# Attention, a dense layer pair and a top-2 mixture of experts on one core: loads, router tables, preparations and score products moved around the first pass

## The chip, the cores and the metric

One core of a Trainium2 chip runs the whole kernel as one program. The metric is device time in microseconds (us) of that program. Several executions are timed and their median counts; one more execution is profiled.

## The reference, cut to what matters

Three stages follow each other: causal attention with a decay (4 batches, 8 heads, 576 tokens, head size 64), a dense layer pair with squared ReLU (2304 tokens, 512 to 2048 to 512), and a router that sends each token to two of eight experts.

```
scores = q @ k.T / 8 + (cum[:, None] - cum[None, :])      # cum = cumsum(log f); causal
x = softmax(scores) @ v                                   # 2304 x 512
x = relu(x @ w_in) ** 2 @ w_out
logits = x @ w_gate + log1p(exp(x @ w_noise)) * noise
for each token: the two best experts, out += weight * (relu(x @ w1[e]) @ w2[e])
```

## The kernel before, in words

Most products run as three half-precision products (high times high, high times low, low times high), so an operand is first split into a high and a low part. ScalarE (ACT) copies the high part and VectorE (DVE) subtracts to get the low part.

**The ramp** is written out by hand: the string PLAN (line 57) is a list of tokens, and each issues one small step; the engines keep that order. It computes the "head" attention, which is the first two blocks of 128 queries of each batch, cut into 12 subs (numbered j, line 375). Per sub: S (hd_s, line 389) the scores, R (hd_max) the maxima, E (hd_exp) the exponentials, T, C and P the turn and the product with the values, n, h, l and XT the normalized tokens into xT. Subs 0 to 7 stand in PLAN, and j of 8 to 11 run later (hd_tick, line 520). The tokens lw0 to lw7 load the weight blocks of the dense layer on the queue of SyncE (SP), LW8 to LW11 on that of GpSimd (POOL); each is 1 MB and goes into one of two buffers (tag "w64"), which comes free when the block is converted (ca, cb, cc, ch, cl: conv_shift to conv_low, lines 549 to 568).

**The passes** (line 1087) are the dense layer. A pass takes one chunk c of 384 tokens through some of the 16 weight blocks i: mm1 (line 607) is 12 matmuls into the one PSUM tile m1, then ACT's ReLU, square and second square (lines 594 to 598) and DVE's low part (line 603); mm2 (line 636) is 9 matmuls into three accumulators, two steps later (LAG). Passes 0 and 1 do blocks 0 to 7 of chunks 0 and 1, and their sums are spilled to DRAM (spill, line 624, tiles sp) and fetched again (unspill, line 632, tile bk); passes 2 and 3 do blocks 8 to 15; then the other four chunks follow. Pass 0 is in PLAN (tokens m, r, g, a). From pass 1 on (after line 1086) a scheduler sets the order on every engine. It places instructions by priorities and its own estimates, and `with tc.issue_after(x)` tells it to put what stands inside behind x on the same engine. `pin` holds such instructions.

**In pass 1** hd_tick runs subs 8 to 11 beside the dense layer: hd_s (lines 394 to 412) makes two PSUM banks, one for each half z of the partitions. All its matmuls read 64 rows: z = 0 reads partitions 0 to 63, z = 1 partitions 64 to 127. The program writes them in turn, z = 0, z = 1, and so on. hd_split (line 496) then issues a transposing DMA (tile pt, line 504), and hd_pv16 (line 517) multiplies with the values.

**The rest of the attention** runs as 48 units (att_tick, line 954) beside passes 2 to 6. Before a pair of heads p of batch b can be used, load_qk (line 104, tile qkr, 896 KB, two buffers) and load_v (line 98, tile vr, 320 KB) fetch it on SP, and prep and prep_v (lines 192 and 207) split it: three ACT instructions (lines 199, 200, 212), three on DVE (201, 202, 213), and two small DMAs on POOL (205). Pairs 0 and 1 of batch 0 are loaded in pass 1, steps 4 and 5 (line 1141), but put only behind the last head turn of the ramp (token O7); all four preparations of batch 0 stand in the first ticks, which are in pass 2.

**The router's tables** are made by router_setup (line 673), called in pass 1 at step 1: two loads (wgr, nz), six constants on POOL, and two index tables (ini, ino) that POOL fills and SP writes to DRAM in three DMAs of 1024 short pieces each. Its three tiles and those of spill and of the turns share one set of three buffers (tag "x2").

After the passes, each expert is two layers on TensorE (PE) over gathered tokens.

## Time and profile before

| | |
|---|---|
| median of 3 runs | 962.51 us (961.18 to 967.23) |
| the profiled execution | 968.69 us |
| its span, first to last instruction | 966.6 us |
| mean granted TensorE clock | 0.992 |
| PE busy | 930.9 us |
| DVE, ACT, POOL busy | 569.0, 444.4, 203.9 us |

The first matmul of pass 0 starts at 43.9 us, that of pass 1 at 88.7 us and that of pass 2 at 133.7 us; the passes end at 542 us and the experts follow. A "wait" is idle time of an engine just before an instruction, put down to what ended it. In the timeline a row is a run of equal instructions on one engine: start, length, engine, line, operation, tiles, shape, count, and in brackets the idle time before it. Rows with a "q" behind the engine are the sequencer's DMA issues.

### The profile page before, as it was taken

To read this page: it belongs to the slowest core of one execution; us is meant where nothing else is said; L and a number is where in the kernel's file an instruction comes from. 1 tells how busy PE (TensorE), PEld (TensorE's weight loads), DVE (VectorE), ACT (ScalarE), POOL (GpSimd) and SP (SyncE) were. 2 spreads that over 40 slices of the span, in tenths; PEclk is the share of its full clock that TensorE was granted. 3 is DMA by queue.
4 is the path that set the end of the run, shared out by engine and by line. 5 is a ranking of instruction groups with operands and counts; after the bars stand their busy time and mean duration, and the time that the engine had idled before them with its cause. 6 is when DMAs were issued, how large, how long until landed. Compare 5 with 4: busy or idle time off the path is not lost.

```text
span 966.6 us, 17572 instructions
## 1 busy us (share of the span) xinstructions
PE 930.9 (96%) x6854; PEld 541.6 (56%) x6854; DVE 569.0 (59%) x1253; ACT 444.4 (46%) x990; POOL 203.9 (21%) x247
## 2 busy tenths in 40 slices
PE   6899998998999999999999999999999999999995
PEld 4766554554555555555555444656474747565662
DVE  6888777788788788776464462516262525343220
ACT  4775677777476667655344431324150413232110
POOL 4000011014132032002024025233313141111102
PEclk9999999999999999999999999999999999999999
DMA  8368888798969959735358846696968585741203
GB/s 294 136 241 240 191 214 252 124 212 183 223 133 248 227 101 229 160 52 94 73 189 233 201 123 121 142 211 162 238 157 182 146 196 119 174 97 17 38 12 43
DMA packets 219815, 155.33 MB, mean 161 GB/s; under 512 B 175634, under 2 KB 186258, under 8 KB 217682
## 3 DMA queue, kind: packets, MB, share of 16 engines
q1 hardware_dynamic: 207170, 124.75, 53.4%
q0 software_dynamic: 12416, 29.31, 14.7%
q8 instruction: 55, 0.90, 0.4%
q10 hardware_dynamic: 144, 0.13, 0.1%
q14 instruction: 30, 0.25, 0.1%
HBM read 89.05 MB, written 23.98 MB: 117 GB/s over the span
## 4 chain that ended last, share of the span: by engine, by line
PE 75%; DMA 12%; DVE 6%; issue 5%; ACT 1%; POOL 1%; SPq 0%; POOLq 0%; DVEq 0%; ACTq 0%; another core or an unknown queue 0%
PE e L914 19%; PE e L931 18%; PE acc L642 14%; PE m L587 12%; PE m1s L587 3%; DMA w<-in_w_io_dram 3%; DMA pt<-phl 3%; PE po L322 2%; DMA out_dram<-y,tix 2%; DMA pt<-ph 2%; PE ps L229 1%; PE ps L230 1%; PE po L325 1%; DVE w L557 1%; DMA xgT<-xg 1%
## 5 line engine op out<-in xcount | busy, mean ns | idle before, releaser
L931 PE MATMUL e<-w2s,hT 128*128 128x512 f16 (+1 forms) x960 | 209.5, 379 | 2.4 <-DVE y L934 1.8
L642 PE MATMUL acc<-w,g 128*128 128x512 f16 x864 | 205.8, 379 | 0.8 <-ACT sp L627 0.8
L914 PE MATMUL e<-xgT,w1s 128*128 128x310 f16 (+2 forms) x1536 | 204.9, 294 | 0.8 <-DVE hT L919 0.8
L587 PE MATMUL m<-xT,w 128*128 128x384 f16 x960 | 172.1, 329 | 4.4 <-ACT r L594 3.2
L914 PEld LDWEIGHTS <-w1s 128*128 128x128 f16 x1536 | 139.7, 97 | 64.8 <-issue 1.0
L918 ACT ACTIVATE hT<-e 128x310 f16<-128x310 f32 (+2 forms) x128 | 54.5, 429 | 255.6 <-PE e L914 252.1
L931 PEld LDWEIGHTS <-hT 128*128 128x128 f16 (+1 forms) x960 | 99.5, 104 | 109.1 <-issue 2.1
L587 PEld LDWEIGHTS <-w 128*128 128x128 f16 x1152 | 109.6, 98 | 80.4 <-issue 9.0
L642 PEld LDWEIGHTS <-g 128*128 128x128 f16 x864 | 80.9, 98 | 86.5 <-issue 2.3
L934 DVE TENSOR_SCALAR y<-e,gs 128x512 f32<-128x512 f32 (+1 forms) x40 | 30.0, 750 | 162.9 <-PE e L931 120.9
L919 DVE SCALAR_TENSOR_TENSOR hT<-e,hT 128x310 f16<-128x310 f32 (+2 forms) x128 | 60.2, 478 | 60.9 <-ACT hT L918 60.7
L935 POOL DMA_INDIRECT out_dram<-y,tix x40 | 65.4, 1635 | 141.5 <-DVE y L934 134.2
L796 POOL DMA_INDIRECT table<-ent,si x36 | 43.1, 1199 | 131.0 <-DVE si L793 121.8
L872 POOL DMA_INDIRECT xg<-x2d,tix x40 | 40.7, 1018 | 129.5 <-DMA xgT<-xg 122.9
L258 DVE TENSOR_REDUCE sm<-ps 128x1 f32<-128x384 f32 (+2 forms) x96 | 53.1, 563 | 19.8 <-PE ps L231 10.1
L594 ACT ACTIVATE r<-m 128x384 f32<-128x384 f32 x80 | 39.0, 488 | 53.3 <-PE m L587 50.4
L604 DVE TENSOR_TENSOR r<-r 128x384 f32<-128x384 f32 x64 | 35.4, 554 | 30.6 <-ACT g L595 30.3
L261 ACT ACTIVATE pr<-ps,sm 128x384 f32<-128x384 f32 (+1 forms) x64 | 40.0, 628 | 28.2 <-DVE sm L260 25.4
L595 ACT ACTIVATE g<-r 128x384 f16<-128x384 f32 x96 | 50.1, 522 | 1.8
L837 DVE SCALAR_TENSOR_TENSOR w2s<-wr,w2s 128x1024 f16<-128x1024 f32 x32 | 39.1, 1223 | 17.7 <-ACT w2s L836 17.6
L282 DVE TENSOR_TENSOR phl<-pr,phl 128x384 f16<-128x384 f32 (+1 forms) x64 | 38.7, 620 | 17.2 <-ACT phl L281 14.8
L836 ACT ACTIVATE w2s<-wr 128x1024 f16<-128x1024 f32 x32 | 33.6, 1051 | 27.8 <-DMA wr<-in_w_dram 26.8
(279 smaller groups left out, 1071.6 us busy)
## 6 DMA issues: line engine op xcount, KB each, us to landing
wr<-in_w_dram SPq DMA_DIRECT2D x64, 512.0 KB, 4.1
qkr<-in_qk_dram SPq DMA_DIRECT2D x16, 896.0 KB, 5.9
w<-in_w_io_dram SPq DMA_DIRECT2D x8, 1024.0 KB, 8.4
w<-in_w_io_dram POOLq DMA_DIRECT2D x8, 1024.0 KB
vr<-in_v_dram SPq DMA_DIRECT2D x16, 320.0 KB, 5.2
x2d<-x SPq DMA_DIRECT2D x18, 256.0 KB, 2.6
hraw<-in_qka_dram SPq DMA_DIRECT2D x8, 512.0 KB
out_dram<-zero SPq DMA_DIRECT2D x5, 768.0 KB, 3.9
```

The lines of the kernel that those rows point to most:

```text
L258: seen[u] = nc.vector.tensor_reduce(sm[:, z:z + 1], ps[z][:, :N], AX.X, ALU.max).ins
L261: nc.scalar.activation(pr[:, z, :N], ps[z][:, :N], AF.Exp, bias=sm[:, 2 + z:3 + z], scale=SC_S, accum_out=su[:, p // 2, z, p % 2:p % 2 + 1])
L587: nc.tensor.matmul(ps, W[i][:, wi, 0, 128 * cc:128 * cc + 128], xT[:, xi, cc, r0:r0 + CH], start=(x == 0), stop=(x == 11))
L595: nc.scalar.activation(g[:, 0, :], r, AF.Square, scale=2.0 ** -10)
L642: last[0] = nc.tensor.matmul(acc[t], g[:, gi, 128 * t:128 * t + 128], W[i][:, wi, 1, :], start=(i in ends[c][0] and x == 0), stop=(i in en ...
L796: s_ = nc.gpsimd.indirect_dma_start(out=table, out_offset=bass.IndirectOffsetOnAxis(ap=si[:, t, k:k + 1], axis=0), in_=ent[:, t, k, :], in ...
L872: nc.gpsimd.indirect_dma_start(out=xg, out_offset=None, in_=x2d[0:seen, :], in_offset=bass.IndirectOffsetOnAxis(ap=rows_t[key, j][0], axis=0))
L914: last[0] = nc.tensor.matmul(ps[:, :hw], w1s[:, cc, wi, 128 * i:128 * i + 128], xgT[:, 4 * xi + cc, c], start=(x == 0), stop=(x == 11)).ins
L918: relu[0] = nc.scalar.activation(hi, ps[:, :hw], AF.Relu).ins
L919: nc.vector.scalar_tensor_tensor(hT[:, i, 1, c], ps[:, :hw], 0.0, hi, op0=ALU.max, op1=ALU.subtract)
L931: last[0] = nc.tensor.matmul(ps[:m], hT[:, i, hi, 128 * j:128 * j + m], w2s[:, i, wi, :], start=(i == 0 and x == 0), stop=(i == NFE - 1 an ...
L935: s_ = nc.gpsimd.indirect_dma_start(out=out, out_offset=bass.IndirectOffsetOnAxis(ap=ix[:m], axis=0), in_=y[:m], in_offset=None, compute_o ...
```

## The change

- **hd_s**: the same matmuls, first collected in a list; for j of 8 and more each is put behind the one before it on PE.
- **hd_split** sets pin["sp"] to its transposing DMA, so loads issued after it stand behind the newest turn and not behind O7's.
- **Loads and preparations**: pairs 0 and 1 are still loaded at steps 4 and 5 of pass 1; their preparations and the loads of pairs 2 and 3 now stand at steps 6 and 7 of pass 1. Pairs 2 and 3 are prepared in the first two ticks. The load of batch 1's first pair stays with tick 0.
- **Router tables**: router_setup is cut in two, router_first (loads, constants, first table) at the new token ra behind lw3, router_rest (last table, gate weights) at the new token rb ahead of lw4. The call in pass 1 is gone.
- **unspill**: its load stands behind pin["dve"].

```diff
-h0 P1 ... XT1 E30 P2 cb2 lw3 s2 h1 cc2 T30 E31 S4 n2 l1 C30 T31
-R4 ch2 XT2 C31 ca3 E40 P3 cl2 h2 cb3 T40 lw4 E41 s3 ...
+h0 P1 ... XT1 E30 P2 cb2 lw3 ra s2 h1 cc2 T30 E31 S4 n2 l1 C30 T31
+R4 ch2 XT2 C31 ca3 E40 P3 cl2 h2 cb3 T40 rb lw4 E41 s3 ...
@@ hd_s
+        prev = None
+        for o_, l_, r_, first, end in prods:
+            with ExitStack() as guard:
+                if j >= NPL and prev is not None:
+                    guard.enter_context(tc.issue_after(prev))
+                prev = nc.tensor.matmul(o_, l_, r_, start=first, stop=end, skip_group_check=True).ins
@@ hd_split
-        nc.sync.dma_start_transpose(out=pt...)
+        pin["sp"] = nc.sync.dma_start_transpose(out=pt...).ins
@@ unspill
+        with tc.issue_after(pin["dve"]):
+            nc.sync.dma_start(back[c], part[...])
@@ att_tick
-        if k == 0:
+        if k < 2:
             with tc.issue_after(pin["dve"]), tc.issue_after(pin["act"]):
-                prep(0, 0)
-                prep_v(0, 0)
-            load_qk(0, 2)
-            load_v(0, 2)
-        if k < 3:
-            with tc.issue_after(pin["dve"]), tc.issue_after(pin["act"]):
-                prep(0, k + 1)
-                prep_v(0, k + 1)
+                prep(0, k + 2)
+                prep_v(0, k + 2)
@@ main loop
-        if (n, i) == (1, 1):
-            with tc.issue_after(pin["sp"]), tc.issue_after(pin["pool"]):
-                router_setup()
         if n == 1 and i in (4, 5):
             load_qk(0, i - 4)
             load_v(0, i - 4)
+        if n == 1 and i in (6, 7):
+            with tc.issue_after(pin["dve"]), tc.issue_after(pin["act"]):
+                prep(0, i - 6)
+                prep_v(0, i - 6)
+            load_qk(0, i - 4)
+            load_v(0, i - 4)
```

On SP, in the ramp, the weight blocks 2 to 5 (w64_340, w64_444, w64_521, w64_620) follow each other before:

```order
L543 DMA w64_340<-in_w_io_dram 128x2048
L543 DMA w64_444<-in_w_io_dram 128x2048
L543 DMA w64_521<-in_w_io_dram 128x2048
L543 DMA w64_620<-in_w_io_dram 128x2048
L381 DMA hraw_622<-in_qka_dram 128x1024
```

In the changed kernel the router's loads and its three table writes stand between blocks 3 and 4 (w64_444 and w64_542):

```order
L547 DMA w64_340<-in_w_io_dram 128x2048
L547 DMA w64_444<-in_w_io_dram 128x2048
L683 DMA wgr_446<-in_wgn_dram 128x64
L684 DMA nz_137<-in_noise_dram 128x144
L692 DMA table_82<-ini_449 128x8x8
L692 DMA table_82<-ini_449 128x8x2
L706 DMA table_82<-ino_452 128x8x28
L547 DMA w64_542<-in_w_io_dram 128x2048
L547 DMA w64_641<-in_w_io_dram 128x2048
```

Five DMAs moved ahead of block 4 on SP.

On PE, in pass 1, the scores of sub 10 go into the banks psab_1205 (z = 0) and psab_1206 (z = 1). Before, one bank's matmuls stand together, and the other bank's follow some 70 rows later:

```order
L400 MATMUL psab_1205<-hraw_210,hraw_684 128x128
L400 MATMUL psab_1205<-hraw_684 128x128
L400 MATMUL psab_1205<-hraw_210,hraw_684 128x128
L400 MATMUL psab_1205<-hraw_684 128x128
L405 LDWEIGHTS esel_92
L405 MATMUL psab_1205<-c16_84,esel_92 128x256
L405 LDWEIGHTS esel_92
L405 MATMUL psab_1205<-c16_84,esel_92 128x256
```

Now the two banks take turns; the first product of the sub stands alone, some 90 rows earlier:

```order
L416 MATMUL psab_1206<-hraw_210,hraw_705 128x128
L416 MATMUL psab_1205<-hraw_705 128x128
L416 MATMUL psab_1206<-hraw_705 128x128
L416 MATMUL psab_1205<-hraw_210,hraw_705 128x128
L416 MATMUL psab_1206<-hraw_210,hraw_705 128x128
L416 MATMUL psab_1205<-hraw_705 128x128
L416 MATMUL psab_1206<-hraw_705 128x128
L416 LDWEIGHTS esel_92
L416 MATMUL psab_1205<-c16_84,esel_92 128x256
L416 LDWEIGHTS esel_92
L416 MATMUL psab_1206<-c16_84,esel_92 128x256
```

On ACT, at the turn from pass 1 to pass 2, m_1599 and m_1681 are steps 9 and 10 before (of the 16 blocks, counted from 0). Both first preparations stand in one row between them:

```order
L594 ACTIVATE r<-m_1599 128x384
L595 ACTIVATE g<-r 128x384
L598 ACTIVATE r<-r 128x384
L199 ACTIVATE setk_1636<-qkr 128x1152
L200 ACTIVATE setq_171<-qkr 128x640
L212 ACTIVATE vs<-vr 128x10x64
L199 ACTIVATE setk_1650<-qkr 128x1152
L200 ACTIVATE setq_175<-qkr 128x640
L212 ACTIVATE vs<-vr 128x10x64
L594 ACTIVATE r<-m_1681 128x384
```

In the changed kernel m_1621 and m_1697 are steps 9 and 10. The first preparation stands ahead of step 9's ReLU, and the second between that ReLU and its square, with the third spill copy (sp) behind it:

```order
L199 ACTIVATE setk_1537<-qkr 128x1152
L200 ACTIVATE setq_171<-qkr 128x640
L212 ACTIVATE vs<-vr 128x10x64
L345 ACTIVATE xh<-xs 128x512
L631 ACTIVATE sp<-acc_1186 128x512
L631 ACTIVATE sp<-acc_1190 128x512
L598 ACTIVATE r<-m_1621 128x384
L199 ACTIVATE setk_1579<-qkr 128x1152
L200 ACTIVATE setq_175<-qkr 128x640
L212 ACTIVATE vs<-vr 128x10x64
L599 ACTIVATE g<-r 128x384
L568 ACTIVATE w_1691<-w_1437 128x1024
```

The preparations moved up by about one step, and are cut apart by a ReLU.

## Rows read from the trace of the kernel before

**Rows 1.** The page, busy time of PE, PEld, DVE, ACT, POOL with shares.

```profile
PE 930.9 (96%) x6854; PEld 541.6 (56%) x6854; DVE 569.0 (59%) x1253; ACT 444.4 (46%) x990; POOL 203.9 (21%) x247
```

**Rows 2.** Windows: stretch, length, busy PE, PEld, DVE, ACT, POOL, clock, DMA.

```profile
97.00:135.00 38.00, 35.27 (x279) 20.32 (x278) 30.44 (x49) 24.93 (x59) 5.94 (x17) 1.00 0.93 206
135.00:160.00 25.00, 20.38 (x101) 10.14 (x100) 18.42 (x26) 18.57 (x31) 3.44 (x6) 0.93 0.67 228
156.50:159.80 3.30, 3.30 (x12) 1.54 (x11) 3.30 (x8) 3.27 (x6) 1.12 (x2) 0.50 0.56 145
160.00:245.00 85.00, 81.28 (x755) 45.56 (x754) 70.15 (x190) 63.62 (x156) 15.53 (x20) 0.98 0.90 183
245.00:640.00 395.00, 394.15 (x3166) 214.85 (x3164) 252.77 (x694) 196.25 (x436) 86.25 (x103) 1.00 0.72 160
```

**Rows 3.** Timeline of PE, the six rows with a wait, 76 to 160 us.

```profile
99.99 0.44 PE L517 MATMUL po<-vh,pt 128*128 128x64 f16 x9 [2.06 <-DMA pt<-phl]
...
123.63 0.87 PE L517 MATMUL po<-vh,pt 128*128 128x64 f16 x24 [0.67 <-DMA pt<-phl]
...
142.45 0.81 PE L642 MATMUL acc<-w,g 128*128 128x512 f16 x3 [0.81 <-ACT sp L627]
...
148.92 2.11 PE L587 MATMUL m<-xT,w 128*128 128x384 f16 x12 [1.45 <-ACT r L594]
...
153.76 0.32 PE L230 MATMUL ps<-setk,setq 70*128 70x384 f16 x1 [0.62 <-DMA setk<-c]
...
156.10 3.66 PE L587 MATMUL m<-xT,w 128*128 128x384 f16 x12 [1.74 <-ACT r L594]
```

**Rows 4.** Timeline of PE: scores of sub 7, and one bank of sub 10.

```profile
60.90 1.16 PE L400 MATMUL psab<-hraw 64*128 64x128 f32 x16
...
62.43 2.00 PE L460 MATMUL po<-hv,pth 128*128 128x64 f32 x16
...
93.63 1.16 PE L400 MATMUL psab<-hraw 64*128 64x128 f32 x8
...
95.16 0.82 PE L642 MATMUL acc<-w,g 128*128 128x512 f16 x3
```

**Rows 5.** Timelines of SP and ACT: early loads, first turn, preparations in pass 2.

```profile
81.75 0.43 SPq L107 DMA_DIRECT2D qkr<-in_qk_dram  x1
...
91.56 3.01 SPq L504 DMA_TRANSPOSE pt<-phl  x1
...
143.79 1.15 ACT L199 ACTIVATE setk<-qkr 128x1152 f16<-128x1152 f32 x1
...
148.41 0.47 ACT L594 ACTIVATE r<-m 128x384 f32<-128x384 f32 x1
...
153.88 1.16 ACT L199 ACTIVATE setk<-qkr 128x1152 f16<-128x1152 f32 x1 [3.90 <-DMA qkr<-in_qk_dram]
...
155.58 0.47 ACT L594 ACTIVATE r<-m 128x384 f32<-128x384 f32 x1
```

**Rows 6.** SP, DMA (GB/s in 40 slices of 37 to 44 us), DVE, PE; router tables on SP.

```profile
37.50 0.33 SPq L543 DMA_DIRECT2D w<-in_w_io_dram  x1
...
GB/s 0 0 0 0 0 0 0 0 421 140 0 0 187 94 281 515 374 374 421 468 374 468 374 468 421 328 328 0 0 0 0 0 0 0 0 0 0 0 0 0
...
42.58 0.69 DVE L552 TENSOR_SCALAR w<-w 128x1024 int32<-128x1024 int32 x1
43.18 0.68 DVE L486 TENSOR_TENSOR xT<-psxf,xT 128x512 f16<-128x512 f32 x1
...
43.92 2.11 PE L587 MATMUL m<-xT,w 128*128 128x384 f16 x12 [1.21 <-DVE xT L486]
...
107.80 5.55 SPq L691 DMA_DIRECT2D table<-ini  x2
113.45 3.23 SPq L697 DMA_DIRECT2D table<-ino  x1
```

**Rows 7.** The page, median time of a load from issue to landing (last column).

```profile
qkr<-in_qk_dram SPq DMA_DIRECT2D x16, 896.0 KB, 5.9
```

More of the change, by code (lines that the diff above doesn't have):

```diff
@@ L393, in hd_s @@
         np_ = 4 // (i + 1)
+        v4 = [t.rearrange("p (c w) -> p c w", w=Wd) for t in ps]
+        prods = []
         for p in range(np_):
@@ L399, in hd_s @@
                     r = slice(64 * z, 64 * z + 64)
-                    nc.tensor.matmul(ps[z][:, c], hd["x", b, i][r, 1, pp, :], hd["x", b, kb][r, 0, pp, :],
-                                     start=(p == 0 and kb == 0), stop=False, skip_group_check=True)
+                    prods.append((ps[z][:, c], hd["x", b, i][r, 1, pp, :], hd["x", b, kb][r, 0, pp, :], p == 0 and kb == 0, False))
         for p in range(np_):
@@ L404, in hd_s @@
                 r = slice(64 * z, 64 * z + 64)
-                nc.tensor.matmul(ps[z][:, Wd * p:Wd * p + Wd], decay(r, 4 * b + np_ * a + p, 128), c16[r, 0:Wd],
-                                 start=False, stop=False, skip_group_check=True)
-        v4 = [t.rearrange("p (c w) -> p c w", w=Wd) for t in ps]
+                prods.append((ps[z][:, Wd * p:Wd * p + Wd], decay(r, 4 * b + np_ * a + p, 128), c16[r, 0:Wd], False, False))
         for hf in range(2):
@@ L410, in hd_s @@
                 r = slice(64 * z, 64 * z + 64)
[L411 to L412 removed]
+                prods.append((v4[z][:, :, 128 * i:128 * i + 128], identb[r, hf], masku[r, hf, None, :].to_broadcast([64, np_, 128]), False, hf == 1))
+        prev = None
[4 more added lines that the diff above has]
+                prev = nc.tensor.matmul(o_, l_, r_, start=first, stop=end, skip_group_check=True).ins
         if a == 0:
@@ L633, in unspill @@
         back[c] = astream.tile([128, NT, DM], F32, name="bk", tag="w64", bufs=2)
-        nc.sync.dma_start(back[c], part[CH * c:CH * c + CH, :].rearrange("(t p) d -> p t d", p=128))
+        with tc.issue_after(pin["dve"]):
+            nc.sync.dma_start(back[c], part[CH * c:CH * c + CH, :].rearrange("(t p) d -> p t d", p=128))
     def mm2(c, i):
@@ L671, in attn_moe_moe_kernel, with router_first @@
     pid = consts.tile([128, 1], I32, name="pid")
-    def router_setup():
-        wgr = gpool.tile([128, 4, 16], F32, name="wgr", tag="x2", bufs=3)
+    tab = table.rearrange("(e r) w -> e r w", e=NE)
+    rset = {}
+    def router_first():
+        rset["w"] = wgr = gpool.tile([128, 4, 16], F32, name="wgr", tag="x2", bufs=3)
         nc.sync.dma_start(wgr, wgn)
         nc.sync.dma_start(nz, noise)
-        nc.scalar.activation(wg[:, :, 0, :], wgr, AF.Copy, scale=2.0 ** 7)
-        nc.vector.scalar_tensor_tensor(wg[:, :, 1, :], wgr, 2.0 ** 7, wg[:, :, 0, :], op0=ALU.mult, op1=ALU.subtract)
+        ini = gpool.tile([128, NE, NJ, 2], I32, name="ini", tag="x2", bufs=3)
+        nc.gpsimd.memset(ini, 0)
+        nc.gpsimd.iota(ini[:, :, :, 0], [[0, NE], [128, NJ]], base=0, channel_multiplier=1)
+        rset["o"] = ino = gpool.tile([128, NR, 2], I32, name="ino", tag="x2", bufs=3)
+        nc.gpsimd.memset(ino, 0)
+        nc.gpsimd.iota(ino[:, :, 0], [[1, NR]], base=0, channel_multiplier=NR)
+        for j0, j1 in ((0, NE0), (NE0, NJ)):
+            nc.sync.dma_start(tab[:, 128 * j0:128 * j1, :].rearrange("e (p j) w -> p e (j w)", p=128),
+                              ini[:, :, j0:j1].rearrange("p e j w -> p e (j w)"))
         nc.gpsimd.iota(iota8, [[1, NE]], base=0, channel_multiplier=0, allow_small_or_imprecise_dtypes=True)
@@ L1017, in attn_moe_moe_kernel @@
             nc.scalar.activation(fch[:, 1], fch[:, 0], AF.Ln)
+        elif tok == "ra":
+            router_first()
+        elif tok == "rb":
+            router_rest()
         elif tok == "clamp":
```

27 lines of the change are left out of this document (8 added, 19 removed).

## The prediction

> **What bounds the kernel now.** I read the page first. PE is busy for 930.9 us [rows 1] of a span of 966.6, so nothing off PE can give more than the 36 us that PE is idle. The second view is PE by windows. From 245 to 640 us it misses 0.85 us of 395 [rows 2], so no edit is worth anything there. The stretches that the diff touches are others: 97 to 135 us (2.73 us of idle time, 38.00 less 35.27), 135 to 160 us (4.62 us idle) and 160 to 245 us (3.72 us idle) [rows 2]. The third view, PE's timeline, puts names to the first two. Two matmuls of a turned sub wait 2.06 and 0.67 us for the transposing DMA pt, and from 142 to 156 us there are four waits of 0.81, 1.45, 0.62 and 1.74 us: for a spill copy, twice for ACT's ReLU, and for the small POOL DMA [rows 3]. Right behind the last of them the granted clock is 0.50, which is the 1.2 GHz level, for 3.3 us [rows 2], and a step's twelve matmuls take 3.66 us where those at 148.92 take 2.11 [rows 3]: 1.55 us more, and with the matmuls behind them about 1.7 us. So what can be won by waiting less is 7.35 us of waits and 1.7 us of clock. DVE is busy for 30.44 of 38.00 us there [rows 2], 80%. It has a fifth to spare, and PE's gains end where that is used up.
>
> **Paired scores.** The new order lets the two halves of the partitions take turns on PE. What that is worth stands in one trace: sub 7, whose order is written by hand and is in turns, needs 1.53 us for both banks (60.90 to 62.43). One bank of sub 10, put by the scheduler in one piece, needs 1.53 us alone (93.63 to 95.16) [rows 4]. So two halves in turns take the time of one. Each of subs 9 to 11 has two banks of that kind, three times 1.53 = 4.59 us saved. Sub 8 is already half in turns, and I count 0.9 us for it. Together 5.5 us. The order takes some back: in each sub the first product stands alone, and sub 9 is cut twice more. A product in a piece of its own costs about an eighth of the 1.16 us of eight instructions [rows 4], twice, since it runs as two instructions: 0.29 us. For some four such pieces that is 1.1 us. I take -4.5 us. The ends are -6.1 us (four full subs) and -3.5 us (half of the pieces more, and switches that I do not see). PE is the bound in this stretch, so this counts in full unless DVE cannot follow, and its spare fifth of 38 us, 7.6 us, is just more than this term and the next together.
>
> **Loads behind the turns, tables out of pass 1.** The four early loads leave SP from 81.75 us; the first turn is issued at 91.56 us [rows 5], behind 2.4 MB (two times 896 and 320 KB) that nobody needs before 143.79 us. Its reader on PE waits until 99.99 us [rows 3]. Without them the turn finds free DMA engines. The second wait, 0.67 us, follows a stretch in which SP spends 5.55 and 3.23 us on the table writes [rows 6], now gone from there. I take -2.0 us of the 2.73. The ends are -2.7 and +1: in the new order the second half of the first turn's split stands behind a weight conversion on DVE, which may wait for its own load. The fetch of the spilled sums moves too. It has slack of tens of us before pass 2 ends, so I cost it at nothing. If it came late, the wait would be one of DVE at the end of pass 2, well behind 160 us.
>
> **Preparations.** Before, two whole preparations hold ACT from 143.79 to 148.41 us, 2.31 us each, and the ReLU behind them is late. The third waits 3.90 us for its load, and the ReLU behind it, at 155.58 us, is late again [rows 5]. That is the 1.45 and the 1.74 us, and most of the clock. In the new order each preparation stands in a row of its own, and the third one's load leaves earlier. What is late next? ACT's queue from the end of step 8 on PE: its three activations (1.5 us), preparation 0 (2.31), a turn's high part and two spill copies (1.7), then step 9's ReLU at +5.6 us. PE needs 3.3 us for the rest of pass 1's sums and 1.95 us for step 9, and is there at +5.25. That is nearly even. Then preparation 1 (2.31) stands between this ReLU and its square, so the square is done at +8.9 us, when PE has done step 10's twelve matmuls as well, even again. A weight conversion (1.1), the second square (0.5) and the third spill copy (0.5) end at +11.1, where PE asks for the freed accumulator at +10.3: a wait of 0.8 us. So 0.8 to 1.2 us of waits when the loads are there. They may not be: the last turn leaves SP some 6 us ahead of the end of step 8, the loads queue up behind it, and one takes 5.9 us [rows 7]. So preparation 0 may wait a us or two with ReLU, spill copies and squares queued behind it on ACT, and preparation 1 again. I take 3.5 us of new waits and clock against 4.62 + 1.7 = 6.3 us of old: -2.8 us. The ends are -6.3 us (all gone) and +3 us (both loads some 4 us late).
>
> **Tables in the ramp.** POOL's ten instructions for them fall into its idle time before its first weight load and cost nothing. SP's five DMAs do not. They stand between weight blocks 3 and 4, and the last one waits for a DVE instruction that stands behind block 3's second conversion step, at about 38.6 us. Now block 4 leaves SP at 37.50 us, its bytes end in the 27th slice, at 41.7 us, and DVE takes it up at 42.58 us [rows 6]: 0.9 us of slack. With the last table write in front (at best some 1.3 us of SP's time, a quarter to a half of the 5.55 for two) block 4 leaves at about 40.0 us, lands at about 44.3, and DVE, which also got two small instructions (0.4 us), stands still for about 1.4 us. Behind it stands the low part of xT that the first dense matmul waits for already (1.21 us at 43.92) [rows 6], so the whole kernel shifts. I take +2.0 us. The ends are +0.4 us (the two instructions alone) and +5.5 us (SP held for 3.23 us and more as at 113.45, with a half clock behind the longer wait).
>
> The Trainium skill, DMA: Bandwidth & Descriptors, Queues, rings and completion order, says that on each DMA engine descriptors are consumed in ring order. It speaks against this placing: block 4's bytes then start only behind the table's 1024 pieces on SP's ring. By it the estimate for this term would be some 0.5 to 1 us dearer than by SP's issue time alone; no row before has the two in this order.
>
> **Behind 160 us** the same units run with other waits; 160 to 245 us holds 3.72 us of idle time and another dip of the clock (0.98 mean) [rows 2]. I take 0, with 2 us either way.
>
> **The sum.** -4.5 - 2.0 - 2.8 + 2.0 + 0 = -7.3 us, on the profiled execution's 968.69 us: 961.4 us. The median of the three timed runs is 962.51, 6.2 us below the profiled one, so some of the waits above may be shorter in an ordinary run; I apply the difference to the median: 955.2 us, or 0.8% less. A measurement of this kernel can tell about 1% (9.6 us) from no change.
>
> **Rivals.**
> 1. The waits only move. DVE and ACT have the same work in less time, the preparations' loads are late, and PE waits as long as before in other places. For it: DVE at 80%, ACT's queue above is even at best. Against it: 3.90 us of the old wait was one load issued too late. Then only the pairs and the ramp's price are left: -4.5 + 2.0 = -2.5, about 960.0 us. Chance 0.20.
> 2. All of it comes: pairs -5.5, waits and clock -9.0, ramp +0.4, so -14.1, about 948.4 us. For it: each wait has one named cause, and each is treated. Against it: SP's order in the ramp. Chance 0.18.
> 3. Slower, by the ramp: SP's table writes hold it as long as at 107.80 (5.55 and 3.23 us), block 4 leaves at 43 us or later, PE stands still before the first dense matmul for 5 us more, and the clock falls, 1.7 us. It decides from the point where the delay passes what pairs and turns give, 6.5 us; with a late load before preparation 0 (+3) it ends at 962.51 + 6.7 + 3 - 4.5 = 967.7 us. Against it: there they were queued behind a turn and a weight load, while from 31 to 38 us only one block is under way. Chance 0.07.
> 4. The pairs do not run together (the order is in turns, but the banks or the pieces between keep the halves apart): -4.5 becomes 0, 959.7 us. Sub 7 speaks against it. Counted with rival 1.
>
> The Trainium skill, TensorE: Matmul & The Clock Gate, Part 1, says that the clock gate sets the rate by how busy PE has been lately. Rows at two waits bear on it: behind the 2.06 us at 99.99 the clock stayed, behind the 1.74 at 156.10, third of three waits close together, it fell. By that rule a stall of 3 us at 44 us would cost its 1.7 us more, as an estimate; this is inside rival 3.
>
> **How the numbers follow.** The forecast has 0.55: 955.2 us, its own range 950 to 960. Low end of the range: rival 2, 948, less a little, 947.5; high end: between rivals 1 and 3, 964. Faster by over 1% (below 952.9) takes rival 2 and three tenths of the forecast, 0.34. Slower by over 1% (above 972.1) needs rival 3 at its worst, 0.05. The rest, 0.61, is within 1%.
>
> **What would show it.** Scores: both banks of subs 9 to 11 in one run of rows of about 1.5 us each, and some 4.5 us less of these rows in all. Turns: no PE wait for pt near 100 us. Preparations: ACT's ReLU of steps 9 to 11 not behind two preparations, and no 0.50 window there. Ramp: block 4's issue near 40 us and a DVE wait for it, with the first dense matmul near 46 us instead of 43.92; if it starts at 44.3, that term is wrong, and if PE's waits from 125 to 155 us still sum to 4 us, the third one is.

## The result and the profile after

The changed kernel takes 973.9 us (median of 13 runs, 970.16 to 979.51); the kernel before takes 967.34 in the same comparison (13 runs; the three shown above all lie below that median). The ratio is 1.0076, 95% interval 1.0051 to 1.0101: slower by 0.8%, where 0.8% faster was forecast. The profiled execution took 979.51 us, its span is 977.7.

Where the time went is read first from the moments at which PE starts each stage. A pass starts with the first dense matmul of its first block.

| PE starts | before, us | after, us | late by |
|---|---|---|---|
| pass 0, block 0 | 43.92 | 48.10 | 4.18 |
| pass 0, block 2 | 52.15 | 58.96 | 6.81 |
| pass 1 | 88.67 | 93.81 | 5.14 |
| pass 2 | 133.69 | 138.61 | 4.92 |
| pass 2, block 13 | 161.90 | 166.54 | 4.64 |
| first expert matmul | 542.17 | 549.82 | 7.65 |
| last matmul ends | 956.74 | 968.10 | 11.36 |

All of the loss is there at block 2, before pass 1 begins; 1.67 us of it come back up to pass 1, where the score rows are shorter. The 3.7 us in the experts belong to this one execution: a wait of 5.00 us near 653 us and half the clock beside it. In fourteen of the kernels below that stretch took 412.0 to 415.5 us; before it took 414.6.

The page's line of busy times, after, which answers to [rows 1]: PE's work has hardly changed (the 2.3 us more hold half-clock time).

```profile
PE 933.2 (95%) x6854; PEld 541.7 (55%) x6854; DVE 568.9 (58%) x1253; ACT 445.7 (46%) x990; POOL 204.0 (21%) x247
```

The windows of the kernel after (columns as in [rows 2]): the first blocks of pass 0, pass 1, and pass 2 up to block 13. In the first row there is no PE wait, but the mean clock is 0.75.

```profile
48.10:58.96 10.86, 10.86 (x73) 7.71 (x72) 6.76 (x8) 5.04 (x9) 0.00 (x0) 0.75 0.55 186
...
93.81:138.61 44.80, 40.12 (x308) 21.86 (x307) 39.09 (x59) 31.22 (x73) 5.67 (x8) 1.00 0.69 178
138.61:166.54 27.93, 24.25 (x146) 12.73 (x145) 20.82 (x29) 20.65 (x38) 3.58 (x7) 0.94 1.06 323
...
46.60:53.50 6.90, 5.40 (x20) 3.46 (x20) 4.70 (x5) 1.30 (x3) 0.00 (x0) 0.51 0.29 91
```

The last row finds the place: from 46.60 to 53.50 us the granted clock is 0.51, the 1.2 GHz level. It fell inside PE's wait, before the first dense matmul had begun (the wait ends at 48.10). Blocks 0 and 1 then took 10.86 us instead of 8.23, so the clock cost 2.6 us behind a delay of 4.2.

PE's timeline after, the rows with a wait, which answers to [rows 3]. The first matmuls waited 5.25 us instead of 1.21 and ran 4.00 us instead of 2.11. The 2.06 us for the first turn are gone. In their place stand six shorter waits, for DVE (g), for ACT (r, pr) and for later turns. At 149.58 one wait of 3.62 us for a spill copy replaces four.

```profile
48.10 4.00 PE L591 MATMUL m<-xT,w 128*128 128x384 f16 x12 [5.25 <-DVE xT L490]
113.86 1.68 PE L647 MATMUL acc<-w,g 128*128 128x512 f16 x7 [0.32 <-DVE g L607]
116.50 0.87 PE L521 MATMUL po<-vh,pt 128*128 128x64 f16 x24 [0.95 <-DMA pt<-phl]
120.08 1.04 PE L416 MATMUL psab<-hraw 64*128 64x128 f32 x13 [0.33 <-ACT pr L437]
123.94 2.11 PE L591 MATMUL m<-xT,w 128*128 128x384 f16 x12 [0.66 <-ACT r L598]
128.37 0.82 PE L647 MATMUL acc<-w,g 128*128 128x512 f16 x3 [1.02 <-DVE g L607]
134.66 0.87 PE L521 MATMUL po<-vh,pt 128*128 128x64 f16 x24 [1.41 <-DMA pt<-phl]
149.58 1.44 PE L647 MATMUL acc<-w,g 128*128 128x512 f16 x3 [3.62 <-ACT sp L631]
```

SP's timeline after, in the ramp, which answers to [rows 6]: the last table write goes out at 38.74 us, and weight block 4 at 39.22 instead of 37.50.

```profile
32.00 1.05 SPq L692 DMA_DIRECT2D table<-ini  x2
38.74 0.37 SPq L706 DMA_DIRECT2D table<-ino  x1
39.22 1.52 SPq L547 DMA_DIRECT2D w<-in_w_io_dram  x1
```

DVE's timeline after: it takes block 4 up at 46.76 us instead of 42.58, and the low part of xT, for which PE waits, stands behind it.

```profile
46.76 0.69 DVE L556 TENSOR_SCALAR w<-w 128x1024 int32<-128x1024 int32 x1 [3.91 <-DMA w<-in_w_io_dram]
47.37 0.68 DVE L490 TENSOR_TENSOR xT<-psxf,xT 128x512 f16<-128x512 f32 x1
```

So block 4 was 1.7 us late when it left and 4.2 us late when DVE had it. The bytes show the rest. The row is GB/s from 28 to 48 us, 40 slices of 0.5 us, after; that of before covers 37 to 44 us finer, in [rows 6].

```profile
GB/s 0 0 0 0 0 0 0 197 66 344 393 393 393 340 205 56 39 0 0 0 16 0 0 107 108 7 7 131 98 180 98 213 279 492 377 213 16 0 0 0
```

The two slices of 107 and 108 GB/s, 39.5 to 40.5 us, are the table's 112 KB in 1024 pieces. Block 4 comes behind them, and for 2.5 us at only 98 to 213 GB/s; the full rate is there from 44.5 us.

### The profile page after: what moved, and what is told of

The parts are those of the page before. It is cut to its first block, busy times and chain, and to the rows that moved or that the text cites. A ratio compares the mean times of both kernels' runs of the same rounds, so it can differ in the third digit from the quotient of the medians.

```text
span 977.7 us, 17575 instructions
## 1 busy us (share of the span) xinstructions
PE 933.2 (95%) x6854; PEld 541.7 (55%) x6854; DVE 568.9 (58%) x1253; ACT 445.7 (46%) x990; POOL 204.0 (21%) x247
## 4 chain that ended last, share of the span: by engine, by line
PE 78%; DMA 11%; DVE 5%; issue 2%; ACT 2%; SPq 1%; POOL 1%; POOLq 0%; DVEq 0%; ACTq 0%
PE e L923 20%; PE e L940 18%; PE acc L647 15%; PE m L591 12%; DMA pt<-phl 4%; PE m1s L591 3%; DMA w<-in_w_io_dram 3%; PE po L322 2%; DMA qkr<-in_qk_dram 1%; DMA xgT<-xg 1%; PE ps L229 1%; DMA out_dram<-y,tix 1%; PE ps L230 1%; PE po L325 1%; DVE smh L426 1%
## 5 line engine op out<-in xcount | busy, mean ns | idle before, releaser
L647 PE MATMUL acc<-w,g 128*128 128x512 f16 x864 | 208.1, 382 | 5.1 <-ACT sp L631 3.6
L805 POOL DMA_INDIRECT table<-ent,si x36 | 40.8, 1133 | 130.2 <-DVE si L802 120.8
L846 DVE SCALAR_TENSOR_TENSOR w2s<-wr,w2s 128x1024 f16<-128x1024 f32 x32 | 39.1, 1222 | 14.5 <-ACT w2s L845 12.7
L846 DVE SCALAR_TENSOR_TENSOR w1s<-wr,w1s 128x1024 f16<-128x1024 f32 x32 | 38.8, 1226 | 10.9 <-ACT w1s L845 10.5
```

The source lines that it names most:

```text
L647: last[0] = nc.tensor.matmul(acc[t], g[:, gi, 128 * t:128 * t + 128], W[i][:, wi, 1, :], start=(i in ends[c][0] and x == 0), stop=(i in en ...
L805: s_ = nc.gpsimd.indirect_dma_start(out=table, out_offset=bass.IndirectOffsetOnAxis(ap=si[:, t, k:k + 1], axis=0), in_=ent[:, t, k, :], in ...
L846: nc.vector.scalar_tensor_tensor(lo, t_, sc, hi, op0=ALU.mult, op1=ALU.subtract)
```

## The experiments

The ratio of each kernel is to the kernel before, timed beside it. From its profile I take PE's start of pass 0 block 0 and block 2, and an account of the stretch from block 2 to the first expert matmul, which holds the same work in every kernel: its length, PE's waits in it (the sum of its idle times), the loss by clock (half of the time at clock 0.5), and the rest. One trace each; with ramps that differ, only this stretch is comparable. Half clock that falls into a wait stands in both columns, which makes the rest too small by 1.3 to 1.4 us in e3 and e4 and by 0.8 us or less elsewhere.

| kernel | ratio to before (95%) | block 0 | block 2 | length | waits | clock | rest |
|---|---|---|---|---|---|---|---|
| before | 1 | 43.92 | 52.15 | 490.0 | 11.9 | 3.4 | 474.7 |
| after | 1.0076 (1.0051 to 1.0101) | 48.10 | 58.96 | 490.9 | 14.6 | 5.1 | 471.1 |
| e2 | 1.0027 (1.0001 to 1.0054) | 47.95 | 57.56 | 490.8 | 17.8 | 0.0 | 473.0 |
| f2 | one execution, 972.2 us | 45.65 | 56.27 | 491.9 | 15.6 | 5.1 | 471.2 |
| e4, unpaired | 1.0107 (1.0071 to 1.0143) | 48.28 | 58.70 | 491.2 | 14.8 | 3.4 | 473.0 |
| e1 | 1.0004 (0.998 to 1.0029) | 43.74 | 51.96 | 487.4 | 11.6 | 5.1 | 470.7 |
| f5 | 1.0031 (1.0001 to 1.0062) | 45.67 | 53.90 | 490.4 | 17.2 | 1.7 | 471.5 |
| e3 | 1.0012 (0.9978 to 1.0047) | 43.94 | 52.16 | 494.4 | 17.0 | 6.8 | 470.6 |
| f6, unpaired | 0.9987 (0.9955 to 1.0019) | 43.88 | 52.10 | 491.2 | 14.3 | 1.7 | 475.2 |
| f7 | 0.9991 (0.996 to 1.0022) | 45.36 | 53.59 | 487.8 | 13.1 | 1.7 | 473.0 |
| g1 | 1.0008 (0.9981 to 1.0036) | 44.17 | 52.40 | 486.4 | 12.8 | 1.7 | 471.9 |
| g2 | 1.0015 (0.9991 to 1.0038) | 43.71 | 51.94 | 495.4 | 18.2 | 5.1 | 472.1 |
| g3 | 1.0036 (1.0008 to 1.0065) | 43.73 | 51.95 | 491.6 | 14.6 | 5.1 | 471.8 |
| g4 | 1.0031 (1.001 to 1.0052) | 43.72 | 51.95 | 491.0 | 14.1 | 5.1 | 471.8 |
| h1 | 1.004 (1.001 to 1.0071) | 43.85 | 53.76 | 490.9 | 16.5 | 1.7 | 472.7 |
| h3, unpaired | 1.0017 (0.9987 to 1.0048) | 44.53 | 54.44 | 483.9 | 7.8 | 1.7 | 474.4 |

### The ramp: e2, f2, e4, f5

e2 moves one DMA, the last table's write, behind block 4.

```diff
-... T40 rb lw4 E41 ...
+... T40 lw4 rb E41 ...
```

> The changed kernel with one DMA moved: the write of the last index table (1024 pieces) stands behind weight block 4 on SP instead of ahead of it; the other engines keep their order. Theory A (the loss was made in the ramp: block 4 left SP 1.7 us later and its bytes stood behind the table's pieces, DVE waited 3.91 us, the first dense matmul began at 48.10 us instead of 43.92, and the clock was at half rate for 6.8 us right behind it): the DVE wait for block 4 goes, the first dense matmul begins between 43.8 and 44.6 us, step 2 at 52 to 53 us instead of 58.96, and the time falls by 5 to 8 us against the changed kernel, to 966 to 969 us where the kernel before has 967.3. Theory B (the pieces of all three tables in flight delay block 4, its place on SP does not matter): the first dense matmul stays at 46.5 us or later and less than 3 us come back. Theory C (the loss is made in pass 1 and behind it; what the ramp loses is soaked up there): the first matmul moves as in A, but the time stays within 2 us of the changed kernel's.

The first matmul still waited 3.66 us, and block 0 began at 47.95, of which 1.3 us are an earlier wait of this execution (2.27 us near 23 us, 0.94 in the kernel before). So theory A fails, and B holds for the first matmul; by the ratio 4.7 us came back, more than B's 3. GB/s from 28 to 48 us, e2:

```profile
GB/s 0 0 0 0 0 0 0 0 0 82 131 164 360 410 344 442 254 165 70 3 0 0 0 0 0 16 33 98 131 0 16 295 475 377 426 293 145 38 0 0
```

Block 4 left at 39.06 us and its bytes end in the slices at 45.5 and 46; the table's pieces, issued 1.2 us behind it, come only with its last bytes. Block 4 was nevertheless slow: from issue to DVE 7.5 us, as after. The ratio fell from 1.0076 to 1.0027, and the intervals just touch; in its trace the half clock there lasted 3.4 us, not 6.8.

f2 leaves the first table where it is and takes the last one 30 us away.

```diff
-... T40 rb lw4 E41 ...
+... T40 lw4 E41 ...
-... E70 E71 m4 ca7 cb7 T70 ...
+... E70 E71 m4 ca7 cb7 rb T70 ...
```

> One look. The changed kernel with the last table's write some 30 us later, behind weight block 7; the router's loads and the first table's two writes stay between blocks 3 and 4. With the last table only just behind block 4 the first dense matmul still waited 3.66 us. Theory D (it is the last table's 1024 pieces, given to the same rings 1.2 us after block 4, that hold block 4 even from behind it): now block 4 lands within 5 us of its issue, DVE waits under 0.5 us for it, and the first dense matmul waits 1.2 to 1.6 us. Theory E (it is the first table's 2048 pieces of 8 and 32 bytes, whose completions come 3 to 4 us after their bytes): block 4 still takes over 6.5 us from issue to landing, and the matmul waits over 3 us.

Both numbers of theory E are met, near their edges (over 6.5 us from issue to landing, over 3 us of wait), though the first matmul comes 2.5 us earlier than after. SP, DVE and PE in the ramp of f2:

```profile
37.40 10.89 SPq L547 DMA_DIRECT2D w<-in_w_io_dram  x2
...
44.31 0.69 DVE L556 TENSOR_SCALAR w<-w 128x1024 int32<-128x1024 int32 x1 [1.75 <-DMA w<-in_w_io_dram]
...
45.65 4.00 PE L591 MATMUL m<-xT,w 128*128 128x384 f16 x12 [3.11 <-DVE xT L490]
```

Block 4 left at 37.40, as before, but took 6.9 us to DVE. By its semaphore events it landed in 44.28 - 37.40 = 6.9 us, where the kernel before needs 42.31 - 37.50 = 4.8. So in this one execution the first table alone, whose last bytes left by 37.5 us, cost 2.1 us of landing, 1.9 us of PE's wait (3.11 against 1.21), and half the clock for 6.8 us: 4.1 us at block 2. The last table adds the rest, 2.7 us.

f5 puts all of the tables behind weight block 7.

```diff
-... cb2 lw3 ra s2 h1 ...  T40 rb lw4 E41 ...
+... cb2 lw3 s2 h1 ...  T40 lw4 E41 ...
-... g3 lw7 LW8 cc6 ... m4 ca7 cb7 T70 ...
+... g3 lw7 ra LW8 cc6 ... m4 ca7 cb7 rb T70 ...
```

> The changed kernel with all of the router's tables behind weight block 7 in the ramp, where SP has nothing to load for 18 us and PE is 20 us into pass 0; the order from pass 1 on stays that of the changed kernel. Theory A (the loss was made by tables ahead of block 4): first dense matmul at 43.7 to 44.1 us, step 2 at 52.0 to 52.4, pass 2 at 131 to 133 us (the changed kernel's 138.61 less 6.5), time 5 to 8 us below the changed kernel: 964 to 967 where the kernel before has 966.9. Rival (waits behind the ramp take it back): pass 2 not before 135 us, time within 3 us of the changed kernel's.

The wait before the first matmul is again 1.20 us, the blocks behind it run at full clock (2.11 us):

```profile
45.67 2.11 PE L591 MATMUL m<-xT,w 128*128 128x384 f16 x12 [1.20 <-DVE xT L490]
48.49 2.11 PE L591 MATMUL m<-xT,w 128*128 128x384 f16 x12
```

Block 0 starts at 45.67 only because this execution, too, had the longer wait near 23 us (2.29) with half clock behind it; g1 to g3, with the same ramp, start it at 43.71 to 44.17. The ratio fell from 1.0076 to 1.0031, 4.4 us where theory A had 5 to 8, and the intervals overlap. Pass 2 starts at 134.94 us, or some 133.4 without that early wait, where A had 131 to 133. The loss before the first matmul is given back; a time below the kernel before is not reached.

e4 is the counterpart: the kernel before with only the tables moved into the ramp.

```diff
-        if (n, i) == (1, 1):
-            ... router_setup()
+        elif tok == "ra": router_first()
+        elif tok == "rb": router_rest()
```

> The kernel before with nothing but the router's tables moved into the ramp, at the places the change uses (the scheduler reorders some of pass 1 and 2 as a result). Theory A (the ramp costs 6.8 us by the first dense matmuls, and the DMAs taken out of pass 1 give back at most 0.7 us): first dense matmul near 48.1 us, step 2 near 58.9, time 5 to 7 us above the kernel before. Theory C (pass 1 soaks up what the ramp loses): first matmul at 48.1 us, but the time within 2 us of before.

Theory A held: the first matmul is at 48.28, block 2 at 58.70, and the kernel is 1.07% slower (10 us, where A had 5 to 7). This part of the change alone makes as large a loss as the whole; freed of the tables, the stretch behind it gave nothing back (491.2 us against 490.0).

### The tables in pass 1: e1

The changed kernel with its tables where they were.

```diff
+        if (n, i) == (1, 1):
+            with tc.issue_after(pin["sp"]), tc.issue_after(pin["pool"]):
+                router_first()
+                router_rest()
```

> The changed kernel with the router's tables back in pass 1, at step 1 as before; pairs, loads and preparations stay as changed. Theory A: the ramp is the one of before (first dense matmul at 43.9 us, step 2 at 52.2), and the tables cost pass 1 0 to 1.5 us: time 966 to 969 us, 5 to 8 us below the changed kernel and within 2 us of before. Rival (the tables cost pass 1 as much as they cost in the ramp, their pieces stand before turns and weight loads): ramp as before, but over 5 us lost in pass 1 and 2, and the time within 2 us of the changed kernel.

The ratio is 1.0004: the whole loss is gone, by one part undone. It also says that everything else in the change, together, is worth nothing that these runs can tell: the forecast had -9.3 us for its three terms, the tables' removal from pass 1 among them, and the interval allows -1.9 to +2.8.

The tables may have a price in pass 1 too. In e1 and g4, the two kernels that have them there beside the changed loads, PE waits 4.37 and 4.50 us for ACT's ReLU near 106.6 us, at half the clock for 6.8 us; no other kernel has that wait. What makes the ReLU late was not tried.

### The pairs: e3, f6

e3 is the kernel before with nothing but hd_s of the changed one.

> The kernel before with nothing but the paired scores of subs 8 to 11. Theory A (PE is the bound in pass 1, the pairs take 3.9 us off PE's rows and off the time): score rows of these subs 7.9 to 8.1 us instead of 11.9, and the time 3 to 5 us below before. Rival (DVE and the turns set pass 1, PE only waits more where the scores are shorter): the same score rows, but pass 1 from its first dense matmul to that of pass 2 stays within 1.5 us of 45.02 us, PE's idle time in it grows by 2 to 4 us over 2.73, and the time is within 1.5 us of before.

The score rows shrank (9.3 us, of which 1.3 are half clock, against 11.9), and the time did not. Where it went, e3's PE timeline shows: the turns, still behind the early loads and the tables on SP, are later than before against a PE that is sooner (2.06 and 0.67 us in [rows 3]), and the clock falls beside them.

```profile
100.03 0.32 PE L521 MATMUL po<-vh,pt 128*128 128x64 f16 x5 [3.70 <-DMA pt<-phl]
120.42 0.29 PE L521 MATMUL po<-vh,pt 128*128 128x64 f16 x2 [4.67 <-DMA pt<-phl]
```

Its waits in pass 1 are 8.36 us, so the rival's direction holds; but its pass 1 of 52.19 us was foreseen by neither. It holds these waits and 10.2 us at half the clock; the next five blocks, with 2.35 us of waits and no half clock, took 24.5 us instead of 28.2.

f6 is f5 without pairs.

> The kernel with all tables behind weight block 7, but the scores of subs 8 to 11 not paired, as before. Theory (the pairs take 3.9 us off PE's rows, and most of it comes back as waits for DVE and for the turns in pass 1): score rows of 11.9 us against 8.0, PE's idle time in pass 1 1 to 3 us less than with pairs, and the time 0 to 2 us above the run with pairs. Rival (the pairs count in full): the time 3 to 5 us above it.

0.9987 against 1.0031 with pairs: neither 3 to 5 us above, nor clearly below, since the intervals overlap. The rest without waits and clock is 3.7 us more than in f5, which is the pairs' worth; the waits and the clock are 2.9 us less.

### Preparations and their loads: f7, g1, g4, h1

f7 is f5 with the preparations of pairs 0 to 3 back in the first ticks of pass 2 (att_tick as before, the steps 6 and 7 of pass 1 without them).

> The kernel with all tables behind weight block 7, but the preparations of pairs 0 to 3 and the loads of pairs 2 and 3 back in the first ticks of pass 2, as before. Theory (the spread preparations wait for their loads with the spill copies behind them, 3.7 us at the turn of the passes, and give nothing): the time within 1.5 us of the run with spread preparations, waits from pass 2's first dense matmul to its sixth 3.5 to 5.5 us. Rival (the spread preparations are worth their 2.8 us): the time 2 to 4 us above that run.

0.9991 against 1.0031: not 2 to 4 us worse, rather 0.4% better, though the intervals overlap. Spreading the preparations brought nothing here. A reason stands in the changed kernel's ACT timeline, from 141 to 150 us: preparation 0 waits 3.75 us for a load that left SP at 140.60, and the two spill copies that PE waits for stand right behind it.

```profile
141.84 0.52 ACT L602 ACTIVATE r<-r 128x384 f32<-128x384 f32 x1
146.12 1.16 ACT L199 ACTIVATE setk<-qkr 128x1152 f16<-128x1152 f32 x1 [3.75 <-DMA qkr<-in_qk_dram]
147.19 0.72 ACT L200 ACTIVATE setq<-qkr 128x640 f16<-128x640 f32 x1
147.81 0.72 ACT L212 ACTIVATE vs<-vr 128x640 f16<-128x640 f32 x1
148.44 0.61 ACT L345 ACTIVATE xh<-xs 128x512 f16<-128x512 f32 x1
148.96 1.06 ACT L631 ACTIVATE sp<-acc 128x512 f32<-128x512 f32 x2
```

g1 is f5 with the loads one turn earlier: pin["sp"] is not moved to the last turn.

```diff
-        pin["sp"] = nc.sync.dma_start_transpose(out=pt...).ins
+        turn = nc.sync.dma_start_transpose(out=pt...).ins
+        if j < NSUB - 1:
+            pin["sp"] = turn
```

> The kernel with all tables behind weight block 7, and the loads of pairs 0 and 1 put behind the third turn of pass 1 (sub 10) instead of behind the last (sub 11). With them behind the last turn, preparation 0 waited 3.75 us on ACT for its load in the changed kernel, the second spill copy stood behind it, and PE waited 3.6 to 4.0 us for that copy. Theory (the preparations' own loads are what is late): ACT's wait for the first load falls under 1 us, PE's wait for the spill copy under 1 us, and the time falls by 2 to 4 us against the run with late tables. Rival (the loads were put behind the turn for a reason: 2.4 MB ahead of it make it late): the last turn takes over 12 us from issue to its reader instead of 9, PE waits 3 us or more for it, and the time stays within 1.5 us.

ACT's wait for the first load fell from 4.16 us in f5 to 1.63 (the theory had under 1), PE's for the spill copies from 4.02 to 0.66. The ratio is 1.0008 against 1.0031 (2.2 us, with overlapping intervals), the account 4.0 us shorter. PE's timeline of g1, around the turn of the passes:

```profile
134.28 0.82 PE L649 MATMUL acc<-w,g 128*128 128x512 f16 x3 [0.49 <-DVE g L609]
136.90 3.63 PE L593 MATMUL m<-xT,w 128*128 128x384 f16 x12 [1.79 <-ACT r L600]
...
158.04 0.81 PE L649 MATMUL acc<-w,g 128*128 128x512 f16 x3 [0.66 <-ACT sp L633]
```

g4 makes the same edit on e1.

> The changed kernel with the tables back in pass 1 as before (the best mean ratio so far, 1.0004 of the kernel before), and the loads of pairs 0 and 1 behind the turn of sub 10. Theory (late loads ahead of the preparations are a price of their own, whatever stands around them): 2 to 4 us below that run, so a ratio to the kernel before of 0.995 to 0.998. Rival (DVE's work in pass 1 and the order that the scheduler finds set the time, and an earlier load only moves the wait): a ratio of 0.999 or more.

It came out at 1.0031, not below e1's 1.0004 (the intervals overlap): the rival. The turn that reached PE in time in e1 made it wait 2.81 us here.

h1 joins f7 and g1.

> All tables behind weight block 7, the loads of pairs 0 and 1 behind the turn of sub 10, and the preparations back in the first ticks of pass 2: the two edits that took waits away, together. From step 2 to the first expert matmul the kernel before needs 490.0 us, of which 11.9 are PE's waits and 3.4 the half clock; each edit alone needed 486.4 and 487.8. Theory (the pairs' 3.9 us come out where waits do not grow): 484 to 487 us there, waits and clock together under 14 us, ratio to the kernel before 0.994 to 0.998. Rival (what one edit takes away, the other puts back, as so far): waits and clock over 15 us, ratio 0.999 to 1.003.

The rival again: 1.004, a turn 2.84 us late, spill copies 1.54 and 1.06 us late. Two edits that took waits away, each by itself, brought new ones together.

### DVE's share: g2, g3

g2 is f5 with the conversions of weight blocks 13 and 14 later, g3 is f5 with that of block 15 as early as before (the change moved it; the diff above leaves that line out).

```diff
-WHEN = {(1, 0): 10, (1, 1): 11, (1, 2): 12, (1, 4): 13, (1, 5): 14, (2, 1): 15}
+WHEN = {(1, 0): 10, (1, 1): 11, (1, 2): 12, (1, 5): 13, (1, 7): 14, (2, 1): 15}
```

> The kernel with all tables behind weight block 7, and the conversions of weight blocks 13 and 14 one and two steps later in the order, so that DVE has some 5 us less to do in pass 1 and more in pass 2. Theory (from 105 us on DVE, not PE, sets pass 1: in the chain of waits of the run with late tables 16 us of DVE instructions stand without a gap between a weight block and the last turn): pass 1 gets 2.5 to 5 us shorter than its 45.19 us, PE's waits in it fall from 5.06 to under 2.5 us. Rival (PE's own rows, or the transposing DMAs, set it): pass 1 within 1 us of 45.19 us. The whole time is for neither more than 3 us off, as the work comes back in pass 2.

> The kernel with all tables behind weight block 7, with the conversion of weight block 15 back at the last step of pass 1, where the kernel before has it: the change moved it to the second step of pass 2, which the prediction did not price. Theory (DVE sets the end of pass 1): if the scheduler puts the conversion ahead of the last turn, pass 1 gets 2 to 5 us longer, else the end of pass 1 is the same and only pass 2's first steps change, by under 2 us. Rival (the later conversion is what costs, because pass 2 then has preparations and a conversion together): the waits of pass 2's first five steps fall from 4.86 us to under 2.5 and the time falls by 2 us or more.

Both theories of g2 missed: pass 1 got longer (47.41 against 45.19), the waits in it stayed (5.10). The 1.40 us for the last turn went, and 2.31 us for ACT's ReLU came at 124.97. In g3 the end of pass 1 was the same (45.35 us), so block 15's conversion was priced rightly by silence. DVE's quantity of work is then not by itself what sets pass 1. The chain of waits of the changed kernel from 100 us on suggests what does: a weight load, DVE's instructions for it and for the last sub with next to no gap, and the turn. (Columns: start, length, what; the rows of DVE in the middle are left out.)

```profile
100.44 8.43 DMA w<-in_w_io_dram
...
108.90 0.71 DVE w L556
...
125.51 0.07 DVE w L561
125.58 9.03 DMA pt<-phl
134.61 0.05 issue
134.66 0.87 PE po L521 x24
```

The kernel before has weight loads in the same chain:

```profile
93.69 8.23 DMA w<-in_w_io_dram
...
105.95 6.16 DMA w<-in_w_io_dram
...
121.78 6.75 DMA w<-in_w_io_dram
```

A load on POOL waits until DVE has converted a block and freed its buffer (9.38 us before 100.44, after), and DVE waits for the load (3.91 us before 108.90). PE's rows stand only at the end of the first chain and not in the second, of which 44% are "issue", time in which the profile shows no wait. That this loop holds pass 1 near 45 us is argued and not shown: from the chains, and from nine kernels (44.5 to 45.4 us in before, after, e2, f2, f5, f7, g3, h1 and h3), in which PE's own work in pass 1 is 41.9 and 42.3 us without pairs and 40.0 to 40.1 with them. The other seven of the table took 47.4 to 52.3 us, by longer waits, half clock or both (together 6.8 to 13.5 us). A run with a third buffer, which would try it, was not made.

### Without pairs again: h2, h3

h2 and h3 are g1 and f7 with the scores of before.

> The run with loads behind the turn of sub 10 (486.4 us from step 2 to the first expert matmul, ratio 1.0008), with the scores unpaired. Theory (the pairs are worth 3 to 4 us of PE's own time, in any surroundings; only the waits beside them change with the order that the scheduler finds): the time on that stretch without waits and clock is 3 to 4 us above the 471.9 us of the run with pairs. Rival (the pairs only exchange rows on PE, other rows get longer): it is within 1 us of it. The ratio can be anything from 0.997 to 1.006 by either, as waits change too.

> The run with late tables and preparations back (487.8 us from step 2 to the first expert matmul, 473.0 without waits and clock, ratio 0.9991), with the scores unpaired; so of the change only the order of loads, the late tables and block 15's later conversion are left. Theory as in the run before: 3 to 4 us more without waits and clock, 476 to 477. Rival: within 1 us of 473.0.

h2 came out at 1.0064 (1.0026 to 1.0101); its trace holds a single wait of 21.09 us for the last turn, so its account tells nothing of the pairs. h3's rest is 474.4, 1.4 us above f7: between the two expectations. But with 9.5 us it has the least waits and clock of all, and yet a ratio of 1.0017: one trace does not give the median.

Over all: the rest is 470.6 to 473.0 us in the twelve kernels with pairs, 473.0 to 475.2 in the four without. Means are 471.8 and 474.3: the pairs take 2.5 us off PE's own time in these traces (as much when half clock inside waits is counted once). Waits and clock together are 14.5 to 23.8 us with pairs (mean 19.0) and 9.5 to 18.2 without (mean 14.8). In the traces the waits take what the pairs give. The times do not say more: of the four couples that differ in the pairs alone, two are slower with them (e3 to before 1.0012, f5 to f6 1.0031 to 0.9987) and two faster (f7 to h3 0.9991 to 1.0017, g1 to h2 1.0008 to 1.0064), each with overlapping intervals.

## Why the prediction was wrong

**Tables in the ramp, +2.0 forecast, 6.8 measured at block 2.** This step failed, and it alone turns the sign. Its order was right: the last table in front of block 4, block 4 later, DVE still, the low part of xT behind it. The time at which block 4 leaves was even put too late (40.0, measured 39.22). What failed is "lands at about 44.3": it let the block take as long as before, 4.3 us, though it stood behind 1024 pieces, and it let the first table, done before block 4 leaves, cost nothing. It took 7.5 us; f2 shows that the first table alone makes 2.1 us of that. The "0.9 us of slack" was misread as well: it counts from the last bytes, but by the semaphore events block 4 landed at 42.31 us before, 0.27 us ahead of DVE. And the clock's price stood only in rival 3, with 1.7 us, and at the end of the range: here the half clock of 6.8 us, 1.4 us of it inside the wait, cost 2.6. In the four kernels with a longer wait there (after, e2, f2, e4: 3.11 to 5.47 us) the clock was at half for 3.4 to 6.8 us. The wait is not its only cause, though: in h1 and h3 it was at half for 3.4 us from 44 us on, behind the usual wait of 1.2; in the other eleven with that wait it was not.

Rival 3 came nearest, with a chance of 0.07. Its reason did not come: the last table's write held SP for 0.37 us, and block 4 left at 39.22, not at 43 or later. That its sum for the ramp, 5 + 1.7 = 6.7 us, meets the measured 4.2 + 2.6 = 6.8 is luck. A ramp with almost no slack deserved a larger chance.

The Trainium skill, DMA: Bandwidth & Descriptors, Queues, rings and completion order, was cited for that estimate: descriptors are consumed in ring order. The trace agrees both ways: after, the table's pieces come first and block 4 behind them; in e2, block 4 first and the pieces behind. The 2.1 us of f2 it does not explain by itself, since there all packets of the table had begun by 37.5 us, and block 4's first came at 39.5.

**Pairs, -4.5 forecast.** The rows came: 11.86 us for subs 8 to 11 before, 7.98 in e1, 3.9 us less. A whole sub of two banks now runs in 1.5 us, with the lone first product of 0.42 apart; sub 10 after, first row and the row behind it:

```profile
106.97 1.04 PE L416 MATMUL psab<-hraw 64*128 64x128 f32 x13
...
108.50 0.20 PE L521 MATMUL po<-vh,pt 128*128 128x64 f16 x1
```

Of the 3.9 us, 1.7 lie ahead of pass 1 and counted in full: from block 2 to pass 1 PE needs 36.52 us before and 34.85 after, with no wait in either. The other kernels have the same two figures, 36.5 without pairs and, less waits of up to 1.1 us, 34.9 with them. The other 2.2 lie in pass 1 and did not count, though 24 value products (0.9 us) also moved from there into pass 2. What failed is "PE is the bound in this stretch, so this counts in full unless DVE cannot follow": pass 1 took 45.02 us before and 44.80 after, as its waits grew by 1.95 us. That DVE's spare fifth is no reserve, since it is time in which DVE waits for weight blocks (3.91 us at 108.90), is the reading of the chains, which I had not laid over pass 1; it was not tried by a run.

**Loads behind the turns, -2.0 forecast.** The wait named, 2.06 us, is gone after, and grew to 3.70 in e3, where the loads stay ahead: the mechanism held. But pass 1's waits together went from 2.73 to 4.68 us, by later turns and by g and r. Taking the tables out of pass 1 was worth nothing: e1, with them in, has the lowest ratio of the kernels with all of the change's other parts, though its interval overlaps that of f5.

**Preparations, -2.8 forecast.** Waits from pass 2's start to block 13 went from 4.62 to 3.68, with one stretch of half clock as before, so -0.9 us. The warning in the step was the case: preparation 0 waited for its load with spill copies behind it, 3.75 us, near the forecast's "some 4 us late". That price belonged in the middle, not at the end of the range. Whether the spread is worth anything the times do not tell: f7, without it, lies below f5 (0.9991 to 1.0031), h1, without it, above g1 (1.004 to 1.0008), both with overlapping intervals.

**Behind 160 us, 0 forecast with 2 either way.** From block 13 to the experts the changed kernel takes 3.0 us more in its trace, with two stretches of half clock instead of one. Over the kernels with the same order there this went from 379.8 (f5) to 383.3, so it is no price of the change that these runs can tell.

**Rival 1** (the waits only move) is what happened behind the ramp, save that it let the pairs count in full, and rival 3's price, though not its reason, in the ramp; each was given a chance of its own, and the case with both at once stood nowhere: the delay of rival 3, 6.7 us, with nothing gained behind it, 962.51 + 6.7 = 969.2 us. By the measured ratio it is 962.51 x 1.0076 = 969.8.

## What to carry to other kernels

Small pieces (here 3072 of 8 to 112 bytes) are put where no load with a deadline follows within some microseconds, not where SP happens to be free: free issue time is no free ring. Time taken off the busiest engine counts only in a stretch whose chain of waits runs through that engine; here 1.7 us of shorter matmuls counted where PE had no wait, and 2.2 us in pass 1, whose chain seems to run through weight buffers and turns, bought waits. And where a scheduler orders the rest, one moved edit reorders all, so a part is judged by waits and work apart, never by the sum alone.

## What the runs showed of the hardware that was not expected

A load that starts after a burst of small writes is slow although their bytes are through: in f2 block 4's packets of 8 KB took 1.5 to 1.9 us each in its first 1.5 us, in the kernel before 1.0 to 1.1 us in its first 1.0 us, and 0.31 us later in both (medians of the trace's DMA packets by half a microsecond); its first packet came 2.1 us behind the issue, there 1.0. In time this goes with the completions of the small writes, as theory E of f2 has it: their last semaphore event comes at 40.56 us, 3 us behind their bytes, and block 4's packets take 0.31 us from 41.2 on. After it is 43.34 and 44.1, in e4 43.76 and 44.3, in e2 42.07 and 44.0. That the one causes the other is not shown, and it stays open.

In some executions (e2, f5, f7, h3) PE's wait near 23 us is 2.3 us instead of at most 1.3, with 3.4 to 6.8 us of half the clock right behind it, in code that no kernel here changes; so a start of block 0 that is 1.5 us late is no sign of a change.
